# A chunk's TensorE work in one stretch with the next scores; a bank for each transpose; chunk 8 begun earlier

## The chip, the cores and the metric

The kernel runs on one core of one Trainium2 chip. The metric is the device time of one execution in microseconds (us), as a median over runs. "The kernel before" and "the changed kernel" are the two versions. A ratio is always that of one kernel's fast runs to those of the kernel before, taken in the same rounds on the same chip.

## The reference, cut to what matters

A retention layer runs over 4 sequences of 768 tokens with 8 heads of 64, and its output goes through a two-layer MLP of 512 to 2048 to 512 columns with x·sigmoid(1.702·x) between.

```python
for t in range(S):                                  # retention, per head
    state = gamma * state + einsum('bhd,bhe->bhde', k[:, :, t], v[:, :, t])
    y[:, :, t] = scale * einsum('bhd,bhde->bhe', q[:, :, t], state)
# bridge: x = y as (3072 tokens, 512)
h = x @ w_in
g = h * (1.0 / (1.0 + exp(-1.702 * h)))
out = g @ w_out
```

## The kernel before

The 3072 tokens are 24 chunks of 128, six to a sequence; four chunks are a block of 512 tokens, so there are six blocks. For a chunk, `turn` transposes q and k (on TensorE for chunks 0 to 7, on DVE later), `attend` forms the 128x128 scores of each head and masks them on DVE, and `finish` makes the output y from the old state and the masked scores, and the new state from the update u. The MLP works block by block: a first product (`up0`, `up1` or `up`), then a second (`down`). Chunks of the next block are slipped in between units of a product ("units": 16 matmul records in a first product, 8 in a second), so that TensorE has work while other engines prepare a chunk. The MLP products use seven instead of eight partial products, for which DVE and POOL form sums of operands ("sums of G", "sums of X"). A `tag` in the code names a buffer ("bank" below) that TensorE's results go to; a new tile with the same tag has to wait until the tile before it has been read. TensorE's instructions stay in the order of the program; those of the other engines are ordered by a scheduler when the kernel is built.

```python
def attend(j):
    p = ps_a.tile([P, 2, HP, P], F32, name="pa", tag="pa")
    for hp in range(HP):
        for i in range(2):                          # 64 rows by 128 columns
            r = slice(i * D, (i + 1) * D)
            pe.matmul(p[:, i, hp, :], KT[j][r, hp, :], QT[j][r, hp, :], start=True, stop=True)
    AT[j] = home(j, "at")
    for i in range(2):
        dve.tensor_mul(AT[j][:, i], p[:, i], mask[:, i])
    KT.pop(j)

def finish(j):
    # ... cut
    y = ps_a.tile([P, 2, HP, P], F32, name="py", tag="pa")
    # ... old state times q in quarters of 64x64, then v times masked scores in halves
    dve.tensor_mul(x[:, ...], y[:, :, 0:2, :], rowd...)        # X, the MLP's input
    # ... cut
    u = ps.tile([P, HP, D], F32, name="pu", tag="att")
    # ... kd times v in halves, then the new state

def chunks(m):
    return [s for j in range(m * CB, (m + 1) * CB)
            for s in (lambda j=j: turn(j), lambda j=j: attend(j), lambda j=j: finish(j))]

# block 0's first product, with chunks 4 to 7 between its units
for n, unit in enumerate([(1, p) for p in range(3)] + [(half, p) for p in range(3, NP) for half in range(2)]):
    up0(*unit)                                     # bank "x" or "y" by the unit's column
    if n % 2 == 0:
        narrow()                                   # ScalarE's Abs and DVE's operations on the weights
    if between:
        between.pop(0)()
# ... cut: up1, then for each block m: up(d), and
for n, unit in enumerate(down(m)):
    unit()
    # ... cut
    if between and n % 2:
        between.pop(0)()
        if not between:
            sums_x()                               # POOL: sums of X for the next first product
```

## Time and profile before

| | kernel before |
|---|---|
| time, median of 3 (range) | 714.37 us (713.96 to 715.12) |
| profiled run: time, span, mean granted clock | 712.85 us, 710.8 us, 0.995 |
| TensorE, DVE, ScalarE, POOL busy | 97%, 51%, 18%, 16% |
| one chunk in a second product, beside 48 full records | 3.62 us |

How to read the lines. PE is TensorE, ACT ScalarE, DVE VectorE, POOL GpSimd and SP SyncE; a q behind a name marks the engine's queue. A record is one entry of an instruction in the trace. The first page line gives for each engine the busy time, its share of the span, and the count of instructions. The line of clock has a digit for each of 40 slices. The chain of waits goes back from the last instruction and says which engines carried it. The view of waits lists who waited for whom: total us, times, longest. In the timeline a line is a start, a length, the engine, the source line, the operation, what it writes and reads, and in brackets the idle time before it and what ended it. A length in the timeline reaches to the modelled end of the last record, so neighbours overlap a little; I compare starts with starts. The lines themselves stand in the prediction below.

### The profile page before, as it was taken

Reading aid. Unit: us, or ns where it says so; the run is one execution under the profiler, and the core shown is the slowest. Engines: PE = TensorE matmul, PEld = TensorE weight load, DVE = VectorE, ACT = ScalarE, POOL = GpSimd, SP = SyncE. Lnnn points to the kernel's source line nnn. Section 1 sums busy time; section 2 is a strip of 40 time slices with the busy share of each in tenths; the row PEclk is TensorE's granted clock in tenths of the full one; section 3 lists DMA queues with packets and bytes.
Section 4 is the critical chain, followed back from the end, with each engine's and each line's share of the span. In section 5 each row is a group of like instructions: output and inputs, shape, how many; then the busy total and the mean of one; then the engine's idle time right before and its main releaser. Section 6 shows DMA issues by size and latency. Waiting matters only on the chain.

```text
span 710.8 us, 10300 instructions
## 1 busy us (share of the span) xinstructions
PE 692.4 (97%) x4109; PEld 572.5 (81%) x4109; DVE 363.7 (51%) x520; ACT 126.6 (18%) x197; POOL 111.5 (16%) x99
## 2 busy tenths in 40 slices
PE   6799999999999999999999999999999999999997
PEld 5688885447888888888888888888888888888886
DVE  4989889992612832443732443543345363344241
ACT  2322323311000001331000342000333000233000
POOL 2221010000564403000323000222000130200030
PEclk9899999999999999999999999999999999999999
DMA  9984443420012324101334200324300320000001
GB/s 228 290 213 116 135 147 119 135 35 8 15 46 41 74 46 104 35 0 20 74 60 102 46 0 11 75 47 88 66 1 3 72 45 24 23 1 1 15 1 44
DMA packets 143599, 46.31 MB, mean 65 GB/s; under 512 B 130752, under 2 KB 137408, under 8 KB 143552
## 3 DMA queue, kind: packets, MB, share of 16 engines
q1 hardware_dynamic: 134704, 38.84, 23.7%
q10 hardware_dynamic: 8848, 6.83, 3.1%
q8 instruction: 32, 0.52, 0.3%
q14 instruction: 15, 0.12, 0.1%
HBM read 39.33 MB, written 6.29 MB: 64 GB/s over the span
## 4 chain that ended last, share of the span: by engine, by line
PE 76%; DVE 12%; SPq 7%; issue 2%; DMA 2%; ACT 1%; DVEq 0%; ACTq 0%
PE pd L414 28%; PE px L363 16%; PE py L363 12%; PE ph L324 8%; SPq L132 6%; PE ph L311 6%; PE py L264 3%; DVE G L353 2%; PE pa L245 2%; PE py L262 2%; DVE G L354 1%; DVE G L248 1%; DVE G L352 1%; PE pu L278 1%; DMA k_sq<-in_k_dram 1%
## 5 line engine op out<-in xcount | busy, mean ns | idle before, releaser
L414 PE MATMUL pd<-W,G 128*128 128x256 f32 x1120 | 251.6, 382 | 0.4 <-DVE G L354 0.3
L414 PEld LDWEIGHTS pd<-W,G 128*128 128x128 f32 x1120 | 210.0, 190 | 31.7 <-DVE G L354 1.2
L363 PE MATMUL px<-X,W 128*128 128x256 f32 x512 | 119.0, 379 | 0.0
L363 PEld LDWEIGHTS px<-X,W 128*128 128x128 f32 x512 | 97.3, 190 | 13.2
L363 PE MATMUL py<-X,W 128*128 128x256 f32 x384 | 90.7, 379 | 0.0
L363 PEld LDWEIGHTS py<-X,W 128*128 128x128 f32 x384 | 73.0, 190 | 9.9
L311 PE MATMUL ph<-X,W 128*128 128x256 f32 x256 | 59.7, 388 | 0.0
L324 PE MATMUL ph<-W,W 128*128 128x512 f32 x128 | 55.1, 592 | 0.0
L311 PEld LDWEIGHTS ph<-X,W 128*128 128x128 f32 x256 | 48.3, 193 | 7.3 <-issue 0.2
L235 POOL TENSOR_TENSOR kd<-kn_in,cold 128x512 f32<-128x512 f32 x13 | 13.5, 1042 | 250.6 <-PE pu L278 202.0
L324 PEld LDWEIGHTS ph<-W,W 128*128 128x128 f32 x128 | 24.3, 190 | 30.2 <-issue 29.2
L355 POOL TENSOR_TENSOR G<-G 128x512 f32<-128x512 f32 x20 | 29.1, 1452 | 115.8 <-DVE G L354 113.6
L248 DVE TENSOR_TENSOR at<-pa,mask 128x512 f32<-128x512 f32 x32 | 20.6, 685 | 45.9 <-PE pa L245 45.9
L292 DVE TENSOR_TENSOR G<-G,sg 128x512 f32<-128x512 f32 x48 | 33.1, 689 | 13.7 <-ACT sg L290 13.7
L290 ACT ACTIVATE sg<-G 128x512 f32<-128x512 f32 x48 | 30.3, 631 | 51.3 <-DVE G L373 31.0
L290 ACT ACTIVATE sg<-ph 128x512 f32<-128x512 f32 x32 | 19.1, 597 | 102.3 <-PE ph L311 58.8
L414 PE MATMUL pd<-W,W 128*128 128x256 f32 x160 | 35.6, 380 | 0.4 <-DVE W L354 0.3
L414 PEld LDWEIGHTS pd<-W,W 128*128 128x128 f32 x160 | 30.2, 190 | 5.6 <-DVE W L354 1.2
L373 DVE TENSOR_TENSOR G<-py,p 128x512 f32<-128x512 f32 x16 | 11.1, 692 | 38.1 <-PE py L363 38.1
L401 ACT ACTIVATE u<-pd 128x512 f32<-128x512 f32 x6 | 3.6, 597 | 151.4 <-PE pd L414 151.4
L268 DVE TENSOR_TENSOR X<-py,rowd 128x512 f32<-128x512 f32 x20 | 13.7, 687 | 32.0 <-PE py L264 32.0
L387 DVE TENSOR_TENSOR G<-py,vv 128x512 f32<-128x512 f32 x16 | 11.1, 692 | 25.7 <-ACT vv L384 25.7
(97 smaller groups left out, 643.0 us busy)
## 6 DMA issues: line engine op xcount, KB each, us to landing
v_in<-in_v_dram SPq DMA_DIRECT2D x24, 256.0 KB, 3.9
W<-in_moe_w_in_dram SPq DMA_DIRECT2D x12, 512.0 KB, 5.2
out_dram<-o ACTq DMA_DIRECT2D x24, 256.0 KB, 2.8
W<-in_moe_w_out_dram SPq DMA_DIRECT2D x10, 512.0 KB, 3.7
q_sq<-in_q_dram SPq DMA_DIRECT2D x256, 16.0 KB, 1.8
k_sq<-in_k_dram SPq DMA_DIRECT2D x256, 16.0 KB, 1.7
kn_in<-in_k_dram SPq DMA_DIRECT2D x13, 256.0 KB, 3.3
G<-in_moe_w_out_dram SPq DMA_DIRECT2D x6, 512.0 KB, 3.6
```

Of the source, the lines that this page charges most:

```text
L132: tc.keep_in_program_order(sp.dma_start(t[r0:r0 + C4, hp], src[b, hp + HP * (r0 // D), rows, d0:d0 + C4].rearrange("(s p) d -> p s d", p=C4)))
L245: pe.matmul(p[:, i, hp, :], KT[j][r, hp, :], QT[j][r, hp, :], start=True, stop=True)
L248: dve.tensor_mul(AT[j][:, i], p[:, i], mask[:, i])
L262: pe.matmul(out, old[k, s, :], qt[k, s, :], start=(s < 2), stop=False, skip_group_check=True)
L264: pe.matmul(out, vn[:, HP * r + s, :], a[:, r, s, :], start=(not c and s < 2), stop=(s >= 2), skip_group_check=True)
L290: act.activation(s, h, AF.Sigmoid, scale=1.702)
L292: dve.tensor_mul(g, h[:, i], s[:, i])
L311: pe.matmul(h[:, ab], w, X[:, 2 * half + c // 2, c % 2, :], start=(ab == 0 and c == 0), stop=(c == 3), skip_group_check=True)
L324: pe.matmul(h, w, X1[:, c // 2:4:2, c % 2, :], start=(c == 0), stop=(c == 3))
L355: pool.tensor_sub(a[1], a[1], a[0])
L363: pe.matmul(acc[:, u, :], W1[:, 2 * d + u, sa, c, :], X[:, sb, c, :], start=(start and u == 0 and c == 0), stop=(stop and c == 1), skip_gr ...
L414: pe.matmul(p0[:, n, :], g1(m, p, sa)[:, n * P:(n + 1) * P], W2[:, sb, p, :], start=(new and p == 0 and n == 0), stop=(last and p == NP - ...
```

## The change

Its intent is to interrupt TensorE's full-array stream once for each chunk and not twice. The scores of a chunk are cut into quarters of 64x64 and put directly ahead of the output of the chunk before. The update u moves into the bank of y, and so frees the bank that transposes and u had shared; y gets a bank pair apart from the scores, and the transposes take a "y" bank of the products. Chunk 8 is turned and scored in block 0's second product already, so that from then on each visit does one chunk's scores and another's output.

```diff
# ... two hunks cut: loads split by kind
# ... a hunk cut: loads split by kind, a bank tag as an argument
@@ -207,7 +207,7 @@
         at = ["qT", "kT", "kd", "at"].index(name)
         shape = [[HP, P], [HP, P], [H, D], [2, HP, P]][at]
         if j >= 2 * CB:
-            return one.tile([P] + shape, F32, name=name, tag=name)
+            return one.tile([P] + shape, F32, name=name, tag=name, bufs=2 - (at > 0))
         if at < 3:
             t = G[:, at, j % 2 * 2:j % 2 * 2 + 2]
             return t.rearrange("p s t -> p (s t)").rearrange("p (a b) -> p a b", a=shape[0])
@@ -215,11 +215,12 @@
 
     def turn(j, between=lambda: None):
 
+        early = j < 2 * CB
         for name, store in (("q", QT), ("k", KT)):
             t = home(j, name + "T")
-            if j < 2 * CB:
+            if early:
                 x = QKV["kn", j] if name == "k" else QKV.pop(("q", j))
-                p = ps.tile([P, HP, P], F32, name="pt", tag="att")
+                p = ps.tile([P, HP, P], F32, name="pt", tag="y")
                 for hp in range(HP):
                     pe.transpose(p[:, hp, :], x[:, 2 * hp:2 * hp + 2, :].rearrange("p i d -> p (i d)"), ident)
                 act.activation(t, p, AF.Copy)
@@ -228,25 +229,44 @@
                 tc.keep_in_program_order(dve.transpose(
                     t.rearrange("p h t -> p (h t)"), QKV.pop((name, j)).rearrange("p h s d -> p (h s d)")))
             store[j] = t
-        if j % NC < NC - 1:
-            KD[j] = home(j, "kd")
-            x = QKV.pop(("kn", j)).rearrange("p h d -> p (h d)")
-            x = x.rearrange("p (s r d) -> p r s d", s=HP, r=2) if j < 2 * CB else x.rearrange("p (r s d) -> p r s d", r=2, s=HP)
-            pool.tensor_mul(KD[j].rearrange("p (r s) d -> p r s d", r=2), x,
-                            cold[:, H:2 * H].rearrange("p (r s) -> p r s", r=2)[:, :, :, None].to_broadcast([P, 2, HP, D]))
-        if j % CB < 2 or j + 2 < 2 * CB:
-            load(j + 2, "qk" if j + 2 < 2 * CB else "qkv")
-
-    def attend(j):
-        p = ps_a.tile([P, 2, HP, P], F32, name="pa", tag="pa")
-        for hp in range(HP):
+        if early:
+            decay(j)
+        if j + 2 < NCH and (j + 2 < 2 * CB or not early):
+            load(j + 2, "qk")
+
+    def decay(j):
+
+        if j % NC == NC - 1:
+            return
+        KD[j] = home(j, "kd")
+        x = QKV.pop(("kn", j)).rearrange("p h d -> p (h d)")
+        x = x.rearrange("p (s r d) -> p r s d", s=HP, r=2) if j < 2 * CB else x.rearrange("p (r s d) -> p r s d", r=2, s=HP)
+        pool.tensor_mul(KD[j].rearrange("p (r s) d -> p r s d", r=2), x,
+                        cold[:, H:2 * H].rearrange("p (r s) -> p r s", r=2)[:, :, :, None].to_broadcast([P, 2, HP, D]))
+
+    def attend(j, f=None):
+
+
+        if j is not None:
+            p = ps_a.tile([P, 2, HP, P], F32, name="pa", tag="pa")
+            kt, qt = KT.pop(j), QT[j]
+            for hp in range(HP):
+                for h in range(2):
+                    for i in range(2):
+                        r, t = slice(i * D, (i + 1) * D), slice(h * D, (h + 1) * D)
+                        pe.matmul(p[t, i, hp, :], kt[r, hp, t], qt[r, hp, :], start=True, stop=True)
+        if f is not None:
+            finish(f)
+        if j is not None:
+            AT[j] = home(j, "at")
             for i in range(2):
-                r = slice(i * D, (i + 1) * D)
-                pe.matmul(p[:, i, hp, :], KT[j][r, hp, :], QT[j][r, hp, :], start=True, stop=True)
-        AT[j] = home(j, "at")
-        for i in range(2):
-            dve.tensor_mul(AT[j][:, i], p[:, i], mask[:, i])
-        KT.pop(j)
+                dve.tensor_mul(AT[j][:, i], p[:, i], mask[:, i])
+            if j > 2 * CB:
+                decay(j)
+        if f is not None and f + 2 < 2 * CB:
+            load(f + 2, "v")
+        if j is not None and 2 * CB < j < NCH - 1:
+            load(j + 1, "v")
 
     def finish(j):
         c = j % NC
@@ -254,7 +274,7 @@
         vn, a, qt = QKV.pop(("v", j)), AT.pop(j), QT.pop(j)
 
 
-        y = ps_a.tile([P, 2, HP, P], F32, name="py", tag="pa")
+        y = ps_a.tile([P, 2, HP, P], F32, name="py", tag="py")
         where = [(y[s % 2 * D:(s % 2 + 1) * D, r, s // 2, :], s, r) for s in range(HP) for r in range(2)]
         if c:
             for out, s, r in where:
@@ -263,23 +283,21 @@
         for out, s, r in where:
             pe.matmul(out, vn[:, HP * r + s, :], a[:, r, s, :], start=(not c and s < 2), stop=(s >= 2),
                       skip_group_check=True)
+        if c < NC - 1:
+
+            kd = KD.pop(j)
+            u = y[:, 0, 2:4, :].rearrange("p o t -> p (o t)").rearrange("p (s d) -> p s d", s=HP)
+            for s in range(HP):
+                for r in range(2):
+                    pe.matmul(u[r * D:(r + 1) * D, s, :], kd[:, HP * r + s, :], vn[:, HP * r + s, :],
+                              start=False, stop=True, skip_group_check=True)
         half, t0 = divmod(j % CB * P, TH)
         x = X1 if j // CB == 1 else X
         dve.tensor_mul(x[:, 2 * half:2 * half + 2, :, t0:t0 + P], y[:, :, 0:2, :],
                        rowd.rearrange("p (r o) t -> p r o t", r=2))
-        if j + 2 < 2 * CB:
-            load(j + 2, "v")
-        if c == NC - 1:
-            return
-        kd = KD.pop(j)
-        u = ps.tile([P, HP, D], F32, name="pu", tag="att")
-        for s in range(HP):
-            for r in range(2):
-                pe.matmul(u[r * D:(r + 1) * D, s, :], kd[:, HP * r + s, :], vn[:, HP * r + s, :],
-                          start=(s == 0), stop=True, skip_group_check=True)
         if c == 0:
             dve.tensor_copy(new, u)
-        else:
+        elif c < NC - 1:
             pool.tensor_mul(new, old, whole.rearrange("p a b -> p (a b)")[:, :, None].to_broadcast([P, HP, D]))
             dve.tensor_add(new, new, u)
 
@@ -302,9 +320,9 @@
     def g1(m, p, s):
         return g(m, p // 2 * 2, s)[:, p % 2]
 
-    def up0(half, p):
-
-        h = ps.tile([P, 2, TH], F32, name="ph", tag="xy"[p % 2])
+    def up0(half, p, tag):
+
+        h = ps.tile([P, 2, TH], F32, name="ph", tag=tag)
         for ab in range(2):
             for c in range(4):
                 w = W1[:, p, 2 * ab + c // 2, c % 2, :]
@@ -474,10 +492,10 @@
     pool.affine_select(out=m3, in_=m3, compare_op=ALU.is_ge, fill=0.0, base=0,
                        pattern=[[0, H], [1, P]], channel_multiplier=-1)
 
-    def chunks(m):
-
-        return [s for j in range(m * CB, (m + 1) * CB)
-                for s in (lambda j=j: turn(j), lambda j=j: attend(j), lambda j=j: finish(j))]
+    def chunks(first, last):
+
+        return [s for j in range(first, last + 1)
+                for s in (lambda j=j: turn(j), lambda j=j: attend(j, j - 1))]
 
     keep_warm(7)
     turn(0, lambda: keep_warm(3))
@@ -490,17 +508,20 @@
         if j == 0:
             for _ in range(2):
                 fetch()
-        finish(j)
+        if j < CB - 1:
+            attend(None, j)
+        else:
+            attend(j + 1, j)
         if j == 0:
             narrow()
         else:
-            up0(0, j - 1)
-    between = chunks(1)[1:]
+            up0(0, j - 1, "x")
+    between = chunks(CB + 1, 2 * CB - 1) + [lambda: attend(None, 2 * CB - 1)]
     for n, unit in enumerate([(1, p) for p in range(3)] + [(half, p) for p in range(3, NP) for half in range(2)]):
-        up0(*unit)
+        up0(*unit, "xy"[n % 2])
         if n % 2 == 0:
             narrow()
-        if between:
+        if n in (0, 2, 4, 6, 8, 9, 11):
             between.pop(0)()
     for f in range(NFF):
         up1(f)
@@ -509,23 +530,29 @@
         if f >= NFF - 4:
             sums_w2(2 * (f - NFF + 4))
         if f >= NFF - 2:
-            load(2 * CB + f - NFF + 2)
+            load(2 * CB + f - NFF + 2, "qkv" if f == NFF - 2 else "qk")
     for m in range(NB):
-        between = chunks(m + 1) if 0 < m < NB - 1 else []
+        between = []
+        if m == 0:
+            between = [lambda: turn(2 * CB), lambda: attend(2 * CB), lambda: turn(2 * CB + 1)]
+        elif m == 1:
+            between = [lambda: (decay(2 * CB), load(2 * CB + 1, "v"))] + chunks(2 * CB + 1, 3 * CB)[1:]
+        elif 1 < m < NB - 2:
+            between = chunks((m + 1) * CB + 1, (m + 2) * CB)
+        elif m == NB - 2:
+            between = chunks((m + 1) * CB + 1, NCH - 1) + [lambda: attend(None, NCH - 1)]
         if m > 1:
             for d in range(NP // 2):
                 up(d)
-                if m + 1 < NB and d < 2:
-                    load((m + 1) * CB + d)
         for n, unit in enumerate(down(m)):
             unit()
             if m == 0 and n < NP // 2:
                 sums_w2_t3(2 * n)
             if m == 1 and n % 8 == 3:
                 sums_w1(n // 4)
-            if between and n % 2:
+            if between and n % 3 == 2:
                 between.pop(0)()
-                if not between:
+                if m and not between:
                     sums_x()
 
 
```

## The prediction

> **What bounds the kernel now.** I read the page first: busy shares, clock, chain.
>
> ```profile
> PE 692.4 (97%) x4109; PEld 572.5 (81%) x4109; DVE 363.7 (51%) x520; ACT 126.6 (18%) x197; POOL 111.5 (16%) x99
> ...
> PEclk9899999999999999999999999999999999999999
> ...
> PE 76%; DVE 12%; SPq 7%; issue 2%; DMA 2%; ACT 1%; DVEq 0%; ACTq 0%
> ```
>
> TensorE is busy for 97% of the span and carries most of the chain; the next engine has 51%. Only the start is different: in the table of stretches, DVE is busy 18.24 of 20 us from 10 to 30 us and 14.05 of 15 from 30 to 45, because it narrows the weights. From 45 us on, TensorE works almost without a gap, so what shortens its stream shortens the kernel. Second, the view of waits on TensorE (who waits for whom: us in total, times, longest):
>
> ```profile
> PE py L262 <- DVE G L248: 6.1, 5, 2.8
> ...
> PE pa L245 <- DVE X L268: 1.1, 1, 1.1
> ...
> PE py L262 <- DVE at L248: 0.7, 4, 0.2
> ```
>
> The products on the old state (L262) wait for the masked scores (L248). Asked for 44 to 165 us alone, the view shows 0.9 us in two of the five waits on G; the other 5.2 fall in the first 44 us. The 0.7 in four waits on at come after 200 us. Third, the timeline of one chunk in block 1's second product (start, length, engine, line, operation):
>
> ```profile
> 249.30 1.16 PE L245 MATMUL pa<-qT,kT 64*128 64x128 f32 x16
> ...
> 250.40 3.72 PE L414 MATMUL pd<-W,G 128*128 128x256 f32 x16
> ...
> 254.05 0.67 PE L262 MATMUL py<-qT,state 64*64 64x128 f32 x16
> ...
> 254.64 1.15 PE L264 MATMUL py<-at,v_in 128*64 128x128 f32 x16
> ...
> 255.57 0.69 PE L278 MATMUL pu<-v_in,kd 128*64 128x64 f32 x16
> ...
> 256.18 7.17 PE L414 MATMUL pd<-W,G 128*128 128x256 f32 x32
> ...
> 263.29 1.16 PE L245 MATMUL pa<-qT,kT 64*128 64x128 f32 x16
> ```
>
> A chunk interrupts the full-array stream twice: with its scores (64 rows by 128 columns), then, 16 records later, with its output in quarters (L262) and halves (L264, L278). One period is 263.29-249.30 = 13.99 us. It has 48 full-array records, each of which takes 0.216 us in an undisturbed stretch (8 in 1.73 in the chain's px and py pieces), 10.37 in sum. So a chunk costs 3.62 us, and 24 of them some 87.
>
> **What the Trainium skill says.** "TensorEngine Tiling (Array Packing)", Tiling Modes, Key Properties: changing the tiling mode, not just the tile, drains TensorE. The trace agrees, from the starts of single records: the last full record to the first score is 309 ns instead of 216, the first score pair takes 214 ns instead of 112, from the last pair to the full array are 208 instead of 112, and the first full record takes 320. That is 93+102+96+104 = 395 ns for one visit. "PSUM — Partial Sum Buffer", PSUM bank collisions: two engines must not access one bank in the same quadrant at once. That explains why the update u, now put into y's first bank, stands ahead of DVE's read of y. The trace of before has u in its own bank and doesn't show this. "TensorE: Matmul & The Clock Gate", Architectural detail: ScalarE's queue is strict FIFO. The trace agrees around 92 us, below: two finished transposes wait behind a weight operation.
>
> **The change, part by part.** The order of the built programs, with the producer of each semaphore wait looked up, gives the places.
>
> (a) *One stretch.* The scores become 16 products of 64x64 instead of 8 of 64x128, so 32 records instead of 16. Four quarters run side by side: the 16 records of L262 come in fours, 7 ns apart, every 109 ns. 8 groups of 109 are 0.87 us, against 8 pairs of 112, 0.90. So quarters are not faster themselves; they take the mode of L262, and the scores join it without a drain. Saved: 0.395 + 0.02 = 0.415 us for a chunk with a state. For chunks 6, 12 and 18 (first of a sequence, no L262) the switch from quarters to halves is new, 110+51 = 160 ns, which leaves 0.25. Of the 24 chunks, 19 finishes (3 to 6, 8 to 22) are joined with the next scores: 16 x 0.415 + 3 x 0.25 = **7.4 us less**.
>
> (b) *Distance.* The masked scores are now used a whole stretch later, so the waits of L262 after 44 us end: **1.6 us less** (0.9+0.7).
>
> (c) *A bank for each transpose.* q and k of a turn now go to the two "y" banks, and every second unit of block 0's first product uses them too. The built program says: the unit after the turns of chunks 5, 6 and 7 waits for ScalarE's copy of qT. All three turns follow an even unit, where ScalarE first has the sigmoid and the weight's Abs. Before, at chunk 7:
>
> ```profile
> 91.08 0.60 PE L224 MATMUL pt<-ident,q_in 128*128 128x128 f32 x4
> 91.33 0.60 ACT L290 ACTIVATE sg<-ph 128x512 f32<-128x512 f32 x1 [4.64 <-PE ph L311]
> ...
> 91.52 0.60 PE L224 MATMUL pt<-ident,kn_in 128*128 128x128 f32 x4
> 91.82 1.16 ACT L188 ACTIVATE W<-G 128x1024 f32<-128x1024 f32 x1
> ...
> 91.95 2.54 PE L311 MATMUL ph<-X,W 128*128 128x256 f32 x11
> ...
> 92.87 1.08 ACT L225 ACTIVATE G<-pt 128x512 f32<-128x512 f32 x2
> ```
>
> TensorE went on at 91.95, as the transposes had other banks. The first copy ends near 92.87+0.60 = 93.47, and with some 0.08 for the semaphore the unit would start at 93.55: 1.6 us lost, three times, **4.8 us more**. It is the largest loss that I expect.
>
> (d) *The start.* Chunk 4's scores come right after its transposes and wait for the copy of kT: 42.40 plus 0.1 instead of 42.24, 0.3 more. X of chunks 1 and 2 is now multiplied after u. Before, DVE had it 0.34 and 0.46 us after it wanted it, already waiting; u ends 0.3 to 0.85 later. DVE is the bound there; I take 0.7. The 1.1 us wait of L245 on L268 goes (banks of their own), but chunk 1's output waits on DVE's queue at 20.8 us as before, so I count nothing. Sum: **1.0 more**.
>
> (e) *Chunk 8 early.* Its scores move into block 0's second product, one visit for one visit. DVE gets two pairs of transposes and two masks there; it was idle 11.96 us ahead of that product's first output. The sums of G follow closely (TensorE lost some 0.9 us there, from 185.56 to 193.38: 7.81 us for 32 records worth 6.91). I count 0. In block 1, the sums of X now follow chunk 12's decay, which follows a load behind some 34 us of queue issues (8 to 9 us for 16 small transfers); my margin is under 1 us, so 0.2.
>
> Sum: 714.4 - 7.4 - 1.6 + 4.8 + 1.0 + 0.2 = **711.4 us**.
>
> **Rivals.** *The transposes do not wait* (other bank order, or ScalarE free earlier): then 4.8 falls away, 706.6. For it: before, TensorE never waited there. Against: the built program has these three waits by name. *The new waits take everything*: 714 to 715. For it: SyncE's queue is heavily used, loads of a chunk take about 17 us of issue for every 13.6 us of product, and DVE is 85% busy (55.84 of 66) from 44 to 110 us, so each late mask or multiply holds a bank. Against: loads run two chunks ahead, through the first products too. *DVE is the bound up to 165 us* (50.99 of 55 in the last part): gains there vanish, but (c)'s losses then partly too, as DVE catches up while TensorE waits. It would give 708 to 712. *The clock*: the trace grants half clock in two windows of 3.4 us near 22 and 32 us (mean 0.91 and 0.89 in those stretches). One window more or less is up to 1.7 us.
>
> **Range and chances.** Gains after 165 us are sure, 5.9 + 0.7: 13 x 0.415 + 2 x 0.25, and the late waits. What is uncertain lies before 110 us, between 5 lost and 2 gained, beside 1.5 for the clock. So 707.0 to 714.5. 2% is 14.3 us; all joined visits, waits and clock windows together are less. Faster by over 2%: 0.02; within: 0.97; slower: 0.01.
>
> **What would show it.** A stretch's period in blocks 2 and 3 should be 3.2 us over its 48 full records; no wait of the state product on masks after 44 us; three waits of the first product's unit on ScalarE's copy, about 1.6 us each; the first product's end (start of L324's stretch, 109.9 us) some 3 to 4 us later, and everything from there to the end 6 to 7 us shorter. I am wrong if scores in quarters go slower than 109 ns for four, if the waits on the copies are short, or if a load or the sums of X stop TensorE in blocks 1 to 4.

## The result, and the profile after

The changed kernel took 712.39 us (711.51 to 712.99, 4 runs), beside 714.32 us for the kernel before (713.96 to 715.12, 4 runs). The ratio is 0.9971, with a 95% interval of 0.9953 to 0.9988. The output is correct.

The page of the changed kernel, busy shares and chain of waits:

```profile
PE 685.9 (96%) x4493; PEld 572.1 (80%) x4493; DVE 361.3 (51%) x520; ACT 126.5 (18%) x197; POOL 111.1 (16%) x99
...
PE 81%; DVE 9%; SPq 5%; DMA 2%; issue 2%; ACT 1%; ACTq 0%; DVEq 0%
```

TensorE has 6.5 us less busy time (692.4 before), in spite of 384 more records (24 chunks times 16). The prediction expected 7.4 us of the joined visits; the start, where records ran at different clocks in the two runs, is in this number too. But the span is no shorter in this run (711.2 against 710.8; the profiled run of the kernel before took 712.85 us, less than all four timed ones), so what was gained is now spent on waiting. The view of waits on TensorE shows on what:

```profile
PE ph L329 <- ACT G L226: 4.1, 3, 1.4
...
PE pd L432 <- DVE W L372: 1.9, 1, 1.9
...
PE pa L257 <- DVE G L263: 1.7, 1, 1.7
...
PE px L381 <- ACT p L388: 1.2, 1, 1.2
```

L329 is the unit of block 0's first product that waits for ScalarE's copy of a transpose: the three waits that the prediction named. L432 is block 0's second product, waiting for the sums of G. L257 is chunk 4's scores. L381 is block 2's first product. The waits of the state product on masks after 44 us (L262 before, L282 now) are gone. One chunk in block 1's second product, in the timeline:

```profile
245.27 1.10 PE L257 MATMUL pa<-qT,kT 64*64 64x128 f32 x32
246.19 0.62 PE L282 MATMUL py<-qT,state 64*64 64x128 f32 x16
...
248.28 10.63 PE L432 MATMUL pd<-W,G 128*128 128x256 f32 x48
258.83 0.89 PE L257 MATMUL pa<-qT,kT 64*64 64x128 f32 x24
```

The chunk now stands in one piece of 3.01 us to the next full record, and 48 full records follow without a break. The period is 258.83-245.27 = 13.56 us against 13.99: 0.43 us less for a chunk. Dividing both traces at the same places gives a ledger (us, from starts of TensorE's records, D to the modelled end of the last one):

| stretch | before | after |
|---|---|---|
| A: chunk 3's scores to block 0's second product | 125.37 | 128.73 |
| B: second products of blocks 0 and 1 | 111.87 | 112.42 |
| C: block 2's first product | 48.35 | 49.80 |
| D: from block 2's second product to the end | 381.58 | 375.38 |
| sum | 667.17 | 666.33 |

D shows the change as it was meant: 6.20 us less, of which about 1 us is a chunk's visit that moved forward into B. A, B and C give back 5.4 us. In B alone, block 0's part grew by 2.46 (1.27 for chunk 8's scores, the rest a wait) and block 1's shrank by 1.90.

### The profile page after: what moved, and what is told of

It is laid out like the page before. It is cut to its first block, busy times and chain, and to the rows that moved or that the text cites. A ratio compares the mean times of both kernels' runs of the same rounds, so it can differ in the third digit from the quotient of the medians.

```text
span 711.2 us, 11031 instructions
## 1 busy us (share of the span) xinstructions
PE 685.9 (96%) x4493; PEld 572.1 (80%) x4493; DVE 361.3 (51%) x520; ACT 126.5 (18%) x197; POOL 111.1 (16%) x99
## 4 chain that ended last, share of the span: by engine, by line
PE 81%; DVE 9%; SPq 5%; DMA 2%; issue 2%; ACT 1%; ACTq 0%; DVEq 0%
PE pd L432 34%; PE px L381 15%; PE py L381 11%; PE ph L342 8%; PE ph L329 5%; SPq L132 5%; PE py L284 3%; PE pa L257 3%; PE py L292 1%; PE py L282 1%; DVE G L371 1%; DVE W L198 1%; DVE G L263 1%; DMA W<-in_moe_w_in_dram 1%; DMA kn_in<-in_k_dram 1%
## 5 line engine op out<-in xcount | busy, mean ns | idle before, releaser
L432 PE MATMUL pd<-W,G 128*128 128x256 f32 x1120 | 247.4, 381 | 0.4 <-DVE G L372 0.3
L432 PEld LDWEIGHTS pd<-W,G 128*128 128x128 f32 x1120 | 211.3, 190 | 30.6 <-DVE G L372 1.2
L381 PE MATMUL px<-X,W 128*128 128x256 f32 x512 | 119.1, 379 | 1.2 <-ACT p L388 1.2
L381 PEld LDWEIGHTS px<-X,W 128*128 128x128 f32 x512 | 97.1, 190 | 14.9 <-POOL X L356 1.6
L381 PE MATMUL py<-X,W 128*128 128x256 f32 x384 | 90.7, 379 | 0.0
L381 PEld LDWEIGHTS py<-X,W 128*128 128x128 f32 x384 | 73.0, 190 | 9.9
L329 PE MATMUL ph<-X,W 128*128 128x256 f32 x256 | 57.9, 383 | 4.8 <-ACT G L226 4.1
L329 PEld LDWEIGHTS ph<-X,W 128*128 128x128 f32 x256 | 47.8, 190 | 12.3 <-ACT G L226 4.8
L244 POOL TENSOR_TENSOR kd<-kn_in,cold 128x512 f32<-128x512 f32 x13 | 13.6, 1044 | 237.5 <-PE py L292 182.4
L432 PE MATMUL pd<-W,W 128*128 128x256 f32 x160 | 35.6, 380 | 1.9 <-DVE W L372 1.9
L432 PEld LDWEIGHTS pd<-W,W 128*128 128x128 f32 x160 | 30.2, 190 | 7.0 <-DVE W L372 2.3
L423 DVE TENSOR_TENSOR o<-pd,vv 128x512 f32<-128x512 f32 x12 | 7.7, 687 | 35.6 <-ACT vv L419 35.6
```

The costliest lines, as they stand in the source:

```text
L244: pool.tensor_mul(KD[j].rearrange("p (r s) d -> p r s d", r=2), x, cold[:, H:2 * H].rearrange("p (r s) -> p r s", r=2)[:, :, :, None].to_b ...
L329: pe.matmul(h[:, ab], w, X[:, 2 * half + c // 2, c % 2, :], start=(ab == 0 and c == 0), stop=(c == 3), skip_group_check=True)
L381: pe.matmul(acc[:, u, :], W1[:, 2 * d + u, sa, c, :], X[:, sb, c, :], start=(start and u == 0 and c == 0), stop=(stop and c == 1), skip_gr ...
L432: pe.matmul(p0[:, n, :], g1(m, p, sa)[:, n * P:(n + 1) * P], W2[:, sb, p, :], start=(new and p == 0 and n == 0), stop=(last and p == NP - ...
```

## The experiments

Every experiment starts from the changed kernel. Since the times of one kernel scatter by up to some 6 us, I give the ratio with its interval and, for what is smaller than that, the stretches A to D of the ledger from the run's trace. Each run's output was correct. The ledgers together:

| run | ratio to before (95%) | A | B | C | D |
|---|---|---|---|---|---|
| changed kernel | 0.9971 (0.9953 to 0.9988) | 128.73 | 112.42 | 49.80 | 375.38 |
| changed kernel again | 0.9991 (0.9967 to 1.0015) | 127.84 | 114.12 | 49.26 | 375.30 |
| banks x, x, y, y | 0.9931 (0.9907 to 0.9956) | 123.88 | 114.10 | 49.27 | 375.31 |
| turn first | 0.9938 (0.9918 to 0.9959) | 125.68 | 112.42 | 49.07 | 375.29 |
| apart again | 1.0039 (1.0021 to 1.0056) | 128.72 | 113.86 | 48.35 | 379.21 |
| scores in halves | 1.0001 (0.9975 to 1.0027) | 129.44 | 113.36 | 48.35 | 377.38 |
| chunk 9 later | 0.9944 (0.9926 to 0.9961) | 128.72 | 111.19 | 48.94 | 375.30 |
| decay after sums | 0.9957 (0.9933 to 0.9981) | 127.84 | 114.11 | 49.11 | 375.30 |
| both waits away | 0.9973 (0.9952 to 0.9994) | 128.73 | 112.42 | 49.30 | 375.96 |
| unit first | 1.0015 (0.9990 to 1.0041) | 133.12 | 112.43 | 50.04 | 375.48 |
| both, outputs late | 0.9963 (0.9946 to 0.9980) | 128.73 | 112.42 | 48.34 | 375.52 |
| all together | 0.9880 (0.9863 to 0.9896) | 123.01 | 111.19 | 48.34 | 375.31 |
| all, chunk 4 apart | 0.9868 (0.9844 to 0.9892) | 123.49 | 111.20 | 48.35 | 375.30 |

The three B of 114.1 and the A of "unit first" hold stretches at half clock, told of below.

### The changed kernel again: how far a single time can be trusted

No edit.

> The changed kernel once more, unaltered, beside the two that follow on the same chip, as their yardstick. On record: ratio to before 0.9971. The times of one kernel on the other chip spread by some 4 us in steps of about 1.7 us (a half-clock window more or less near the start), so I expect 0.995 to 0.999 here, and from chunk 3's scores to the end 665.5 to 668.5 us in the trace, as in the first (666.3).

Measured: 712.88 us (708.50 to 715.11, 6 runs), ratio 0.9991, beside 713.80 for the kernel before. Before chunk 3's scores the runs differ by up to 4 us. The table of stretches shows the granted clock as the last but two of its columns; in this run's line for 190 to 210 us

```profile
190.00:210.00 20.00, 18.13 (x77) 15.28 (x76) 8.09 (x9) 0.60 (x1) 11.39 (x9) 0.91 0.16 26
```

TensorE was granted 0.91 of its clock. Asked in steps of 1 us, that is one window of 3.4 us at half clock, shortly after the wait of 1.9 us on the sums of G. It is the whole 1.70 us by which B exceeds the first run's B, and the first run had the same wait but no window. Counted in this way, the profiled runs hold none to six such windows each, one to three of them in a row, most from 20 to 37 us. The Trainium skill, "TensorE: Matmul & The Clock Gate", Part 1: The HAM clock gate, says that the gate looks at how busy TensorE was, in free-running windows of 3413 ns, and gives half clock after an idle one. The length agrees, and so does that the same kernel meets them in one run and not in the next. But the window before need not be an idle one. Divided at the clock's own changes into windows of 3.41 us, the 14 traces have 21 windows at full clock with half clock after them, and TensorE was busy for 12.7% to 48.5% of each; of the some 2,770 with full clock after them, the least busy one has 49.7%. In this run the wait lay inside one window (195.02 to 198.43 us, TensorE busy for 45%); in the first run a border cut it, and the window from 197.00 to 200.42 has 51%. This is read from the traces, with busy as the profile counts it; no run set where the windows fall. So a ratio can be off by one or two times 1.7 us, 0.24% each, and experiments on waits of about 1 us have to be read in the trace.

The two runs also differ in the wait of chunk 4's scores. It was 1.68 us in the first, for DVE's mask; here it is

```profile
43.45 1.10 PE L257 MATMUL pa<-G 64*64 64x128 f32 x32 [0.80 <-ACT G L226]
```

0.80 us, for ScalarE's copy of chunk 4's kT, since the mask was done earlier. That is the 0.89 us by which A is shorter here.

### The waits on ScalarE's copies: other banks

```diff
-        up0(*unit, "xy"[n % 2])
+        up0(*unit, "xxyy"[n % 4])
```

> The changed kernel, with one thing different: in block 0's first product the units take their banks in the order x, x, y, y instead of x, y, x, y, so that the unit that follows the turns of chunks 5, 6 and 7 gets an x bank and no longer waits for ScalarE's copy of qT (in the changed kernel 1.32, 1.37 and 1.37 us). Theory of the prediction (TensorE is the bound, the waits on the copies are pure loss): those three waits vanish from the view of waits and the time falls by 4.1 us against the changed kernel, ratio to the kernel before about 0.991. Rival (DVE is the bound up to 165 us, and catches up while TensorE waits): the waits vanish but come back as waits of later units on DVE, and the time falls by under 1 us, ratio 0.996 to 0.997.

Measured: 709.42 us (706.62 to 710.80), ratio 0.9931. The three waits are gone: the view of waits from 44 to 170 us has one line left, the 1.7 us of chunk 4's scores. A fell from 128.73 to 123.88 us, by 4.85. The view of waits had counted 4.06 for the three, from the modelled ends of the records. From starts, the changed kernel needs 1.92, 1.97 and 1.97 us from a turn's second group of transposes to the unit, instead of 0.44, and loses 4.54. B rose by 1.68, and that is a half-clock window behind the wait in block 0's second product. So by time the gain is 0.40% or 2.9 us, and by the trace of A slightly more than expected. Nothing of it came back as a wait on DVE up to 170 us; the rival is refuted.

### The same waits: ScalarE's order

```diff
         up0(*unit, "xy"[n % 2])
+        if n in (0, 4, 8):
+            between.pop(0)()
         if n % 2 == 0:
             narrow()
-        if n in (0, 2, 4, 6, 8, 9, 11):
+        if n in (2, 6, 9, 11):
             between.pop(0)()
```

> The changed kernel with the banks left as they are, but the turns of chunks 5, 6 and 7 are put ahead of the narrowing that stands at the same place, so that ScalarE does sigmoid, copy, copy, weight operation instead of sigmoid, weight operation, copy, copy. Theory of the prediction (the wait is there because the copy stands behind the 1.13 to 1.16 us of the weight operation in ScalarE's queue): the three waits shrink by about 1.15 us each to 0.2 us, 3.4 us less than the changed kernel, ratio to before about 0.992. Rival (the copy itself, or the bank, is slow to come free whatever ScalarE does first): the waits stay above 1 us and the time does not move. Second rival (DVE is the bound there; the weight operation is now 1.2 us later, and the narrowing behind it on DVE with it): no gain or a loss of 1 to 3 us.

This asks why the copy is late. In the changed kernel, around chunk 5's turn:

```profile
55.07 0.60 PE L225 MATMUL pt<-ident,kn_in 128*128 128x128 f32 x4
...
55.32 1.13 ACT L188 ACTIVATE W<-W 128x1024 f32<-128x1024 f32 x1
...
56.34 1.08 ACT L226 ACTIVATE G<-pt 128x512 f32<-128x512 f32 x2
...
56.99 3.29 PE L329 MATMUL ph<-X,W 128*128 128x256 f32 x14 [1.32 <-ACT G L226]
```

The transposes of q are done, but ScalarE first takes the weight's Abs (L188, 1.13 us) and only then the copies; TensorE goes on when the first copy is done. With the order turned, the view of waits has

```profile
PE ph L329 <- ACT G L226: 1.0, 3, 0.3
```

in place of 4.1, 3, 1.4: three waits shortened by 1.03 us each. The ratio is 0.9938, A fell by 3.05. The later narrowing cost TensorE nothing. Both experiments say the same: the wait is the weight operation ahead of the copy, and it becomes a loss because the unit wants the bank that the copy still reads.

### The two visits: apart again

```diff
-        if f is not None:
-            finish(f)
-        # ... masks, decay, loads
+        def rest():
+            if f is not None:
+                finish(f)
+            # ... masks, decay, loads, as before
+        if j is not None and f is not None and j > 2 * CB:
+            late.append(rest)          # done after the next unit
+        else:
+            rest()
```

> The changed kernel with 15 of the 19 joined visits undone, those of blocks 1 to 4: the scores keep their 16 products in quarters, but the output of the chunk before follows one unit of 16 full-array records later, so that a chunk again interrupts the full-array stream twice. Theory of the prediction (a visit costs 0.395 us for two changes of mode; quarters themselves cost nothing): 15 x 0.40 = 6 us more than the changed kernel, ratio to before about 1.005, and 48 full records with a chunk take about 13.97 us again. Rival (the gain of the stretch comes from the scores being faster in quarters, or from the masks no longer being waited for): under 2 us more, ratio 0.997 to 1.000.

Measured: 716.55 us (715.63 to 717.16), ratio 1.0039: slower than both kernels. Against the 0.9971 that is 0.68% of 714 us, 4.9 us. One period in block 2's second product:

```profile
355.29 1.10 PE L258 MATMUL pa<-qT,kT 64*64 64x128 f32 x32
356.32 1.99 PE L439 MATMUL pd<-W,G 128*128 128x256 f32 x8
358.25 0.67 PE L289 MATMUL py<-qT,state 64*64 64x128 f32 x16
...
369.21 0.99 PE L258 MATMUL pa<-qT,kT 64*64 64x128 f32 x28
```

369.21-355.29 = 13.92 us, against 13.56: a visit of its own costs 0.36 us. The output follows 8 records after the scores, a unit of a second product, and not 16 as I had written; the count of visits is what matters. D rose by 3.83 for 11 undone joins, 0.35 each. The rival, that the gain comes from the form of the scores or from the masks, is refuted: it would have left the period near 13.6. C is 48.35 here, without the stall; that is taken up with block 2's first product.

### The scores in halves within the stretch

```diff
-                for h in range(2):
-                    for i in range(2):
-                        r, t = slice(i * D, (i + 1) * D), slice(h * D, (h + 1) * D)
-                        pe.matmul(p[t, i, hp, :], kt[r, hp, t], qt[r, hp, :], start=True, stop=True)
+                for i in range(2):
+                    r = slice(i * D, (i + 1) * D)
+                    pe.matmul(p[:, i, hp, :], kt[r, hp, :], qt[r, hp, :], start=True, stop=True)
```

> The changed kernel with the stretch kept, but the scores as the 8 products of 64 rows by 128 columns of the kernel before in place of 16 in quarters, for all 24 chunks. Theory of the prediction (quarters are not faster in themselves, but they share the mode of the state products, so that the one drain between scores and output goes): a stretch takes 0.16 to 0.2 us longer, with 19 of them and 0.02 for each chunk 3 to 4.5 us more than the changed kernel, ratio to before about 1.002. Rival (the position beside each other is all that counts, the form of the scores nothing): under 1 us more, ratio 0.997 to 0.998.

Measured: 714.10 us (710.48 to 716.90), ratio 1.0001. The period:

```profile
352.26 1.16 PE L256 MATMUL pa<-qT,kT 64*128 64x128 f32 x16
353.35 0.67 PE L281 MATMUL py<-qT,state 64*64 64x128 f32 x16
...
366.05 1.16 PE L256 MATMUL pa<-qT,kT 64*128 64x128 f32 x16
```

366.05-352.26 = 13.79 us, 0.23 more than in quarters. From the scores' start to the state product are 1.09 us here and 0.92 in the changed kernel. Sum over A, B and D: +0.71+0.94+2.00 = 3.65 us, as expected; C gave 1.45 back, since the stall there didn't occur in this run, so that the times show only about 2 us. The form of the scores is half of the matter: of the 0.43 us of a chunk some 0.2 come from the join as such (13.99 to 13.79) and 0.23 from sharing the mode of the state product.

### Block 0's second product: chunk 9 later

```diff
-            between = [lambda: turn(2 * CB), lambda: attend(2 * CB), lambda: turn(2 * CB + 1)]
+            between = [lambda: turn(2 * CB), lambda: attend(2 * CB), lambda: None, lambda: None, lambda: turn(2 * CB + 1)]
```

> The changed kernel with one thing moved: in block 0's second product chunk 9's two transposes on DVE come six units later, behind the three sums of G on which TensorE waits, and no longer between the sums of the first and the second pair. Theory: the prediction's count of 0 for chunk 8 and 9 on DVE was wrong by what this wait grew, because the transposes (1.3 us) push the last sums of G into the time in which POOL works too, where DVE's operations of the same kind take 1.6 us instead of 0.7; then the wait of the second product on the sums of G, 1.9 us in the changed kernel, falls to 0.3 to 0.9 us and the stretch of 32 records from 9.04 to about 7.8 us: 1.2 us less, ratio to before 0.995 to 0.996, and the sums of G take 0.7 us each again. Rival (the sums are late since the outputs that feed them are late): the wait stays at 1.9 us. A half-clock window more or less at the start (1.7 us) can hide this in the times, so the stretch in the trace decides.

In the changed kernel chunk 9's transposes stand on DVE after the first sums of G (188.57 to 189.86), and the last of the sums end late, beside POOL:

```profile
193.17 3.26 POOL L373 TENSOR_TENSOR W<-W 128x512 f32<-128x512 f32 x2 [3.10 <-DVE W L372]
...
195.33 1.64 DVE L371 TENSOR_TENSOR W<-W 128x512 f32<-128x512 f32 x1
...
197.01 1.63 DVE L372 TENSOR_TENSOR W<-g,W 128x512 f32<-128x512 f32 x1
...
198.69 1.56 PE L432 MATMUL pd<-W,W 128*128 128x256 f32 x6 [1.87 <-DVE W L372]
```

With the transposes later:

```profile
196.09 1.64 DVE L372 TENSOR_TENSOR W<-g,W 128x512 f32<-128x512 f32 x1
...
197.65 0.70 DVE L229 STREAM_TRANSPOSE qT<-q_sq 128x512 f32<-128x512 f32 x1
...
197.78 1.99 PE L432 MATMUL pd<-W,W 128*128 128x256 f32 x8 [0.28 <-DVE W L372]
```

The wait fell from 1.87 to 0.28 us and B from 112.42 to 111.19, by 1.23. The ratio is 0.9944. So the 1.3 us of transposes ahead of the sums were the loss. One part of my expectation was wrong: not all sums went back to 0.7 us; three of them still took 1.64. The Trainium skill, "SBUF — State Buffer", SBUF: two separate sides, says that a DVE operation with two SBUF inputs and a GpSimd operation that reads SBUF lock each other out for a whole instruction. The traces agree closely: the sum at 195.33 ends 0.54 us after POOL's operation of 194.71 (length 1.72) ends, and the transposes, with one input, take 0.70 and 0.66 us beside POOL. How many sums meet a POOL operation depends on the order, and only the last end counts for TensorE.

### Block 2's first product: one wait away, then both, then both without a new one

In the changed kernel, around the third product of block 2 (the issue on ScalarE's queue is marked ACTq):

```profile
281.82 1.04 POOL L244 TENSOR_TENSOR kd<-kn_in,cold 128x512 f32<-128x512 f32 x1 [27.44 <-DMA kn_in<-in_k_dram]
...
285.27 1.27 POOL L356 TENSOR_TENSOR X<-X 128x512 f32<-128x512 f32 x1
285.57 0.38 ACTq L424 DMA_DIRECT2D out_dram<-o  x1
286.05 0.60 ACT L388 ACTIVATE p<-px 128x512 f32<-128x512 f32 x1 [12.88 <-PE py L381]
...
286.79 1.97 PE L381 MATMUL px<-X,W 128*128 128x256 f32 x8 [1.22 <-ACT p L388]
```

TensorE needs POOL's third sum of X, ready at 286.54, and ScalarE's copy of p, ready at 286.65. POOL's sums stood behind chunk 12's decay (L244), which waited for a load. ScalarE's copy, whose input was ready before 284, stood behind an output's issue at 285.57, although DVE had that output ready at 282.85. In the built program that issue waits for the completion semaphore of another transfer, a load of chunk 14 (semaphore 107 in the trace, for both) that landed at 285.49. So there are two waits with ends 0.11 us apart, and the view names only the last. The second run of the changed kernel names POOL for the same place (0.7 us). The first experiment takes POOL's wait away:

```diff
-            if j > 2 * CB:
+            if j > 2 * CB and j != 3 * CB:
                 decay(j)
 # ... at the end of block 1's second product
-                    sums_x()
+                    sums_x(m == 1)                 # in program order on POOL
+                    if m == 1:
+                        decay(3 * CB, True)        # after the sums
```

> The changed kernel with chunk 12's decay put behind the sums of X on POOL at the end of block 1's second product, so that these sums no longer wait for the late load of chunk 12's k. In the changed kernel the third product of block 2's first product begins 1.22 us late, and two things were ready at almost the same time: the sums of X on POOL (286.54) and ScalarE's copy of p1 (286.65), which stood behind an output's DMA issue. Theory (two equal waits): this alone takes away POOL's, and ScalarE's remains, so the third product is still 0.4 to 1.2 us late and names ScalarE; gain 0 to 0.2 us, ratio to before about 0.997. Rival (POOL's sums are the cause, ScalarE only came last by chance): the wait goes altogether, 1.2 us less.

Measured: 710.54 us, ratio 0.9957. POOL's sums were done at 279.89 us, before block 2 began at 280.95, yet the third product still waited 0.52 us, for ScalarE: as expected of two waits. The size is not conclusive by itself: C differs by 0.5 us between the two runs of the changed kernel.

The second takes ScalarE's as well, by issuing block 1's last two outputs after the copy:

```diff
-            act.dma_start(rows[th, e], o)
+            if m == 1 and (th, e) in ((1, 1), (0, 1)):
+                held.append(lambda: tc.keep_in_program_order(act.dma_start(rows[th, e], o)))
+            else:
+                act.dma_start(rows[th, e], o)
 # ... in up(d), behind p's copy
+        while held:
+            held.pop(0)()
```

> The changed kernel with both waits at the end of block 1 taken away: chunk 12's decay behind the sums of X on POOL, and block 1's last two outputs' DMA issues on ScalarE behind the copy of p1, so that this copy no longer stands behind an issue that waits for a load. Theory (two equal waits): the third product of block 2's first product starts at once, the four records of the second product take 1.73 us from first to next instead of 3.11, the first product takes 48.35 us instead of 49.80, and the time falls by 0.5 to 1.4 us, ratio to before 0.995 to 0.9965. Rival (the stall follows from DVE's queue or from SyncE's backlog by another way): a wait of 0.4 us or more remains there under another name.

Measured: 711.88 us, ratio 0.9973: no gain, and a wait under another name, which is what the rival had expected. The third product started at once, but

```profile
286.12 2.45 ACTq L432 DMA_DIRECT2D out_dram<-o  x2
...
289.78 2.00 PE L384 MATMUL px<-X,W 128*128 128x256 f32 x8 [0.68 <-ACT u L402]
```

the two issues, moved behind the first copy, held the second copy up in the same way, since they wait for loads as before: they went out at 286.12 and 288.19, each 0.02 us after a load with the same semaphore had landed. A further 0.66 us appeared in block 4's first product. So the wait is in the issue, wherever it stands. The third version holds the two issues back until the last copy of the second group of products, some 20 us later (`while held and d`, behind the copy of vv):

> As the run with both waits at the end of block 1 taken away, but block 1's last two outputs are issued on ScalarE only after the last of the three copies of block 2's second group of products, some 20 us later, when the loads whose completion semaphores they share have landed. In the run before, the third product began at once, but the output issues moved behind the first copy and held the second copy up, so 0.7 us of wait came back at the fifth product. Theory (the stall is two waits, POOL's sums behind a late decay, and ScalarE's queue held by output issues that wait for an unrelated load): no wait of the px products on POOL or ScalarE is left there, block 2's first product takes 48.35 us, and the time falls by 0.5 to 1.4 us against the changed kernel of the same call. Rival (something else holds that place, such as DVE or SyncE's backlog): 0.4 us or more remains there.

Measured: 710.45 us (709.48 to 711.98), ratio 0.9963. There is no wait on TensorE from 275 to 300 us, and C is 48.34. In the same call the changed kernel had 0.9991, so 0.28% or 2.0 us less; the traces of the two differ by 0.92 in C, and by the half-clock window of 1.70 in B, which has nothing to do with the edit. The theory of two waits holds: one alone leaves a wait, both without a new one leave none. It also tells why "apart again" and "scores in halves" have no stall without any edit at this place. Counted from the block's first record, the third product can start at 3.45 us; the third sum and the copy were done at 3.05 and 2.99 there, and at 1.79 and 2.58. Wherever the later of the two came after 3.45, the third product began 0.05 to 0.15 us behind it.

### Chunk 4's scores

```diff
         else:
+            up0(0, j - 1, "x")
             attend(j + 1, j)
```

> The changed kernel with chunk 4's joined stretch put behind block 0's unit of 16 records that follows it, so that this unit stands between chunk 3's masked scores and their use. Theory (chunk 3's mask is on DVE's busy queue; the wait of 1.7 us of the joined stretch on it is a loss that the joining made at the start, against 0.59 us before): the wait of the scores on the mask in the view of waits falls from 1.7 us to 0 to 0.3 us; time 1.2 to 1.7 us less, ratio to before 0.9945 to 0.9955. Rival (DVE is the bound until chunk 4 is turned): the wait goes, but the next unit waits for DVE's X or the weights instead, and the stretch from chunk 3's scores to block 0's second product, 128.7 us in the changed kernel, stays within 0.4 us of that.

Measured: 714.87 us (712.09 to 718.30), ratio 1.0015: no gain. Its interval (0.9990 to 1.0041) lies just above that of the first run of the changed kernel, but overlaps with that of the second. A rose to 133.12 in the profiled run, the slowest of the six. The scores no longer wait, but the unit that stood behind the stretch had hidden DVE's multiplication of chunk 3's output into X. The next unit now waits for it, in the view of waits from 44 to 170 us:

```profile
PE ph L329 <- DVE X L296: 3.2, 1, 3.2
```

DVE works there without a pause, from 43.2 us on. In its cause the rival is right: DVE is the bound in this one place, and what TensorE gains it waits for at the next operand. But not all of A's 4.39 us is this wait:

```profile
43.35 3.68 PE L329 MATMUL ph<-X,W 128*128 128x256 f32 x16
...
53.23 6.55 PE L329 MATMUL ph<-X,W 128*128 128x256 f32 x16 [3.20 <-DVE X L296]
```

The same unit takes 2.9 us more after the wait than before it, as TensorE had half its clock from 52.16 to 58.99 us. So 1.5 us are the exchange of a wait of 1.68 us for one of 3.20, and the rest is the clock. In the window before, 48.75 to 52.16 us, TensorE was busy for 38%; that the long wait brought the half clock on fits the count above, but no run shows it by itself.

### All together, and chunk 4 apart

The best version has the banks in the order x, x, y, y, chunk 9 later, the decays behind the sums of X in blocks 1 to 3, and block 1's last outputs late.

> The changed kernel with all that the runs so far showed to be loss taken out: units' banks in the order x, x, y, y in block 0's first product; chunk 9's transposes behind the sums of G; the decay of the chunk of the next block behind the sums of X on POOL in blocks 1 to 3; block 1's last two outputs issued late. Theory (each of these waits is on TensorE's path by itself): 4.1 + 1.2 + 0.5 to 1.2 us less than the changed kernel of the same call, ratio to before 0.987 to 0.991, some 705 to 707 us, faster than both kernels. Rival (DVE is the bound up to 165 us, what is gained before is given back): gain under 2.5 us, ratio 0.993 or more.

Measured: 704.40 us (703.87 to 705.42), ratio 0.9880, against 712.88 us for the changed kernel and 713.80 for the kernel before on the same chip. It is faster than both, by 1.2%. A, B and C are 5.7, 1.2 and 1.5 us shorter than in the first run of the changed kernel; of A's 5.72, 4.85 are what the other banks gave alone, and 0.9 a shorter wait of chunk 4's scores in this run (0.80 us, for the copy of kT as in the second run of the changed kernel).

The last run tests that join with chunk 4's scores by undoing it alone:

```diff
-            attend(j + 1, j)
+            attend(None, j)
 # ... behind the unit that follows
+    attend(CB)
```

> The best version so far with one of its 19 joins undone, that of chunk 3's output with chunk 4's scores: the output comes first, then block 0's unit of 16 records, then the scores (still in quarters). In the built program chunk 4's scores wait for DVE's second mask of chunk 3 because the scores have a single bank; in the changed kernel that wait is 1.68 us, on top of which the output of chunk 3 waits no more. Theory (this join alone loses: 1.68 us of wait in place of 0.59 us, against 0.35 us for the visit): the wait of the scores on the mask goes, the output waits 0.5 to 0.7 us on its masks as in the kernel before, and the stretch from chunk 3's scores to block 0's second product falls by 0.5 to 0.8 us from the 123.0 us of the best version; in the times this is 0.1%, ratio 0.986 to 0.989, so the trace decides. Rival (DVE is the bound there, so that what TensorE doesn't wait for here it waits for at the next X or weight): the stretch stays within 0.2 us of 123.0 us or grows.

Measured: 702.91 us (701.56 to 705.26), ratio 0.9868, but A is 123.49, 0.48 us longer, not shorter. The theory's expectation failed, as its rival allowed. It set the 1.68 us of the changed kernel's first run against a visit; in the best version's own run the wait was 0.80 us, and undoing the join left 0.6 us of waits and added the visit. The profiled run was one of the two lucky ones of four (granted clock 1.000): it has no half-clock window, and begins chunk 3's scores at 37.39 us instead of 40.48. That explains its time, and the two versions can't be told apart by the ratios.

## Why the prediction was right or wrong, point by point

The time (711.4 predicted, 712.39 measured) lies in the range, and the verdict, within 2%, is right. The steps:

- **What bounds the kernel** was right: nearly every wait taken from TensorE after 44 us showed up in its stream at full size.
- **(a) One stretch** was right in size: 0.43 us for a chunk against 0.415. Its split was a bit off: undoing the join costs 0.36 us, not 0.395, and quarters apart from the output are worth 0.07 (13.99 to 13.92), not 0.02.
- **(b) Distance** was right: those waits after 44 us no longer exist. That they were worth 1.6 us was not measured by itself.
- **(c) A bank for each transpose** was right in place, count and cause: three units after the turns of chunks 5, 6 and 7. The view of waits has 1.32, 1.37 and 1.37 us, 4.06 in sum; counted from starts, as the prediction did, it is 4.54 against 4.8. Two experiments show the cause. (The 0.08 us that I put for the semaphore, without saying where from, is 0.05 to 0.06 in the trace.)
- **(d) The start**: the step on chunk 4's scores was incomplete. I let them wait for the copy of kT, 0.3 us longer than the 0.59 of the output before. In three traces (the second run of the changed kernel, decay after sums, all together) they do, 0.80 us. In the other eight with this join they wait 1.6 to 1.7 us, for DVE's second mask of chunk 3, since the scores have a single buffer and nothing separates chunk 3's from chunk 4's. I had looked at what the scores read, not at what they overwrite. In the three, DVE began the first mask 1.35 us after chunk 3's scores began; in the first run of the changed kernel 2.39 us. They are also the traces with a half-clock window between 32 and 38 us, as the trace that I predicted from has one; that this window lets DVE get ahead is an inference. The term on X of chunks 1 and 2 (0.7) stays open: chunk 3's scores begin at 37.4 and 37.5 us in the two traces without a half-clock window at the start, and between 39.0 and 41.4 us in the others.
- **(e) Chunk 8 early** failed twice. "I count 0" for block 0's second product measured 1.23 us, from chunk 9's transposes rather than chunk 8's. I had seen that the sums of G follow closely, with some 0.9 us lost there already, and still put 1.3 us of DVE work ahead of them at no cost. "0.2" for block 1's end measured 0.9 to 1.45 us. I had POOL's sums behind a late load right. I didn't see the second wait, ScalarE's issue of an output behind an unrelated load. (16 small transfers take 7.5 to 9.7 us of issue in the trace of before, not 8 to 9.)
- **The sum.** From the end of block 0's first product on, the prediction had 6 to 7 us less; the trace has 4.2 less. The 2.2 or so that are missing are the two terms of (e). That first product ends 4.7 us later (114.60 us against 109.91), where I had 3 to 4. So it is partly luck that the number came within 1 us: with the two terms of (e) and the mask of (d), 0.8 us, as in the first trace, my sum is about 714 us, and the second ratio, 0.9991, is 713.7 us. In the traced pair of runs the changed kernel is not faster at all (712.99 us against 712.85).
- **Rivals.** That the transposes do not wait is refuted. That new waits take everything came near: A, B and C together took back 5.4 of the 6.2 us that D shows. DVE as a bound up to 165 us is refuted from 54 us on (other banks) and right at 43 to 53 us (unit first). The clock was real, and wider than I had it: none to six windows.

What stays open is why the same kernel has a ratio of 0.9971 in one call and 0.9991 in another. The intervals overlap, and the half-clock windows are large enough to explain it, but no run fixed them.

## What to carry to other kernels

When a change removes interruptions of a bound engine, ask for each operation that moves what it now overwrites as well as what it reads, and which in-order queue holds the one that frees it. Small work put ahead of a sum or a copy on an idle engine costs its full length if that engine's last result is what the bound engine waits for. And a view that names one wait may hide a second that ends a tenth of a microsecond earlier: take both away before judging either.

## What the Trainium skill lacked or had wrong

- "TensorEngine Tiling (Array Packing)", Key Properties, says that a change of mode drains TensorE but not what it costs. Here a visit to another mode and back cost 0.36 to 0.395 us, and quarters instead of halves ahead of a quartered product saved 0.23 us.
- "DMA: Bandwidth & Descriptors", Rules for kernel authors, says to dedicate a semaphore to a DMA, but not what sharing one costs the issuing engine. Here an output whose data was ready at 282.85 was issued at 285.57, after a load with the same semaphore had landed at 285.49. What stood behind it on ScalarE's queue cost TensorE 0.5 us in the run where nothing else was late (decay after sums).
- "SBUF — State Buffer" has the lock between DVE and GpSimd right, and that it lasts for a whole instruction, but gives no times for two such operations. Here sums of 0.68 us took 1.64 beside POOL, POOL's of 1.27 took 1.58 to 1.72, and DVE's transposes stayed at 0.7.
- "TensorE: Matmul & The Clock Gate" has the length of the window right (3.41 us here, one to three in a row). It says that half clock follows an idle window; here every full-clock window in which TensorE was busy for 48.5% or less was followed by it (21 in 14 traces), and none with 49.7% or more. A kernel that is busy for 96% met none to six half-clock windows in a run, each worth up to 1.7 us of 712.
